# Running most of TensorE's attention units as a hardware loop, with wo read in pieces and multiplied at each layer's end

## The chip, the cores and the metric

The kernel runs on one core of one Trainium2 chip. The metric is the device time of one execution in microseconds (us). Executions of one kernel agree within about 0.15%, so a difference of some microseconds in 2600 can be read.

Names: PE is TensorE (matmul), PEld its weight load, DVE is VectorE, ACT is ScalarE, POOL is GpSimd, SP is SyncE, which issues the large loads. A "unit" is the attention of one query over one head of one batch entry: 16384 keys and values of 128 numbers, a K load and a V load of 4 MiB each. There are 64 units in each of two layers.

## The reference, cut to what matters

```python
x = A_x                                   # (2, 1, 576)
for layer in range(2):                    # written out twice in the original
    q = (layernorm(x) @ wq)               # 32 heads of 128
    p = softmax(q @ k_cache^T * Dh**-0.5) # k_cache, v_cache: (2, 32, 16384, 128) bf16
    x = x + (p @ v_cache) @ wo            # wo: (4096, 576)
    x = x + mixer_mlp(layernorm(x))       # w2 (576, 576), w3 (576, 4608), w4 (4608, 576)
# ... cut: the mixer's shifts; with one position they leave only zeros
```

Nearly all bytes are K and V: 252 loads of 4 MiB, because the last two units of layer 0 stay in SBUF and are the first two of layer 1.

## The kernel before

All loads go through a ring in SBUF of 12 slots (192 KiB a partition), in which a K or V tile takes two slots wherever they are free. The K/V tiles can thus be six deep.

```python
def pump(self):                            # Arena: issue loads while there is room
    while self.queue:
        keys, n, src, align = self.queue[0]
        best = self._place(n, align)       # the free place whose last use is oldest
        if best is None:
            return
        # ... cut: wait for the readers of what lies there, issue from SP
```

A unit's work is spread over three engines: PE transposes the first half of K (`turn`), ACT evicts it, PE multiplies it by the query (`score`); DVE takes the dot products of the other half (`dots`); then maxima, exponentials (ACT), and 128 products with V on PE (`weigh`).

```python
for i in range(U):                         # U = 64 units, all unrolled
    for c in range(NCP):                   # 8 chunks
        self.turn(l, i, c)
        # ... cut: score, unit_max and exps of unit i - 1
        if i % n == 1 and c == 6:
            self.load_wo(l, i)             # 2 heads of wo, 288 KB, from ACT's queue
        # ... cut: dots(l, i, ...) on DVE
    self.weigh(l, i - 1, 0)
    # ... cut
    self.weigh(l, i - 1, 1)
    if i % n == 0:
        self.group_out(l, i - 1)           # normalise 4 units, multiply by 2 heads of wo
    self.query_rows(l, i + 1)
    self.row_max(l, i)
```

Each engine's stream is written out in full. For PE that is 128 units of 258 matmuls, and each matmul is two instructions, a weight load and a multiply (x34571 of each in the page below).

## Time and profile before

| | before |
|---|---|
| time | 2614.34 us median of 4 (2614.12 to 2614.65) |
| bytes read | 1097.74 MB, 420 GB/s over the span |
| K/V tile after tile, usual distance of the landings | 9.71 us (4194304 bytes: 432 GB/s) |
| packets of instruction fetch, queue 8 / queue 14 | 270 of 16384 bytes / 38 of 8192 bytes |

These lines are from the page of the kernel before: busy time of the engines, the DMA engines' mean busy share and the rate in 40 slices of the span, the queues (packets, MB, share of 16 engines' span), and the chain that ended last by engine.

```profile
span 2612.6 us, 74231 instructions
PE 1560.5 (60%) x34571; PEld 1466.2 (56%) x34571; DVE 1983.0 (76%) x2751; ACT 1097.5 (42%) x1681; POOL 0.8 (0%) x10
...
DMA  9999999999999999999889999999999999999997
GB/s 409 430 428 429 428 428 428 430 427 428 428 429 427 429 428 429 429 427 430 375 366 431 427 429 427 428 428 427 432 428 427 428 429 429 428 428 429 427 428 307
...
q1 hardware_dynamic: 42600, 1088.32, 97.4%
...
q8 instruction: 270, 4.42, 0.7%
q14 instruction: 38, 0.31, 0.0%
...
DMA 67%; DVE 27%; PE 5%; issue 1%; SPq 0%; ACT 0%; DVEq 0%
```

The transfers bound it. No compute engine is over 76% busy, the DMA engines are nearly always busy, and the chain is mostly transfers. The waits of PE say the same (columns: us in total, times, longest us).

```profile
PE tps L604 <- DMA ring<-in_A_k_cache_dram: 508.7, 117, 9.9
PE ops L682 <- DMA ring<-in_A_v_cache_dram: 209.8, 115, 3.5
PE ops L682 <- issue: 47.1, 25, 3.2
```

The third line is PE waiting for nothing that the profile shows, in the middle of the products with V.

An average over 16 engines hides whether some of them are late. The trace holds 16 landing times for every K and V load, as many as the page counts DMA engines. I read each as the end of one engine's share; the records name no engine, so wherever engines are told apart below, it is read from landing times. Worked out from those records, us after the first of the 16:

```
kernel before            16 landings, us after the first
K, lands at   25.91      0 ... 0.4 (15 engines) | 1.9
V, last of layer 0,
   lands at 1299.29      0.0 0.1 0.3 0.4 0.5 1.0 | 5.4 | 10.9 | 24.8 24.8 24.9 25.0 25.0 26.4 26.9 27.0
V, last of layer 1,
   lands at 2582.13      0.0 0.3 0.3 0.3 0.4 0.8 | 5.0 | 10.1 | 23.5 23.8 24.9 25.1 25.1 25.2 25.3 25.4
```

Six engines are early, one is 5 us late, one 10 us, and eight about 25 us. The lag grows through a layer and is gone after the boundary: the last landing was 3.5 us behind the first for the load that landed at 176.8 us, 8.2 us at 367.6, 13.0 us at 637.8, 19.2 us at 918.4 and 25.8 us at 1199.6 us, and 1.6 us at 1323.5 us, after the boundary. The kernel waits for all 16 landings of a tile (its waits count in sixteens), so it runs at the pace of the eight late ones.

### The profile page before, as it was taken

The numbers are of one execution on the slowest core, as the hardware profiler recorded it, in microseconds if no ns is written. First come the engines' busy times: TensorE is split into PE (matmuls) and PEld (weight loads), VectorE is DVE, ScalarE is ACT, GpSimd is POOL, SyncE is SP. The second block draws the span as 40 slices with busy tenths as digits, with TensorE's granted clock in tenths as the row PEclk, the third lists the DMA queues.
The fourth block names the chain that finished last, engine by engine and source line by source line (L and its number), as shares of the span: only waits on it lengthen the run. The fifth ranks groups of instructions, "written<-read, shape, count | busy, mean of one in ns | idle before, by whom it ended". The sixth has DMA issues, their size and how long they took to land.

```text
span 2612.6 us, 74231 instructions
## 1 busy us (share of the span) xinstructions
PE 1560.5 (60%) x34571; PEld 1466.2 (56%) x34571; DVE 1983.0 (76%) x2751; ACT 1097.5 (42%) x1681; POOL 0.8 (0%) x10
## 2 busy tenths in 40 slices
PE   5655655656565556655567765556655655655565
PEld 4555555655555555555556755555555555555555
DVE  5777877777777777877759887777877777777775
ACT  3434443444344334434335544344434443444342
POOL 0000000000000000000000000000000000000000
PEclk8666666666666666666656666666666666666665
DMA  9999999999999999999889999999999999999997
GB/s 409 430 428 429 428 428 428 430 427 428 428 429 427 429 428 429 429 427 430 375 366 431 427 429 427 428 428 427 432 428 427 428 429 429 428 428 429 427 428 307
DMA packets 51612, 1102.50 MB, mean 422 GB/s; under 512 B 5028, under 2 KB 13288, under 8 KB 17000
## 3 DMA queue, kind: packets, MB, share of 16 engines
q1 hardware_dynamic: 42600, 1088.32, 97.4%
q10 hardware_dynamic: 8704, 9.44, 1.0%
q8 instruction: 270, 4.42, 0.7%
q14 instruction: 38, 0.31, 0.0%
HBM read 1097.74 MB, written 0.00 MB: 420 GB/s over the span
## 4 chain that ended last, share of the span: by engine, by line
DMA 67%; DVE 27%; PE 5%; issue 1%; SPq 0%; ACT 0%; DVEq 0%
DMA ring<-in_A_k_cache_dram 66%; DVE sd L637 17%; DVE prod L634 9%; PE tps L604 3%; PE misc L655 1%; DMA ring<-in_B_w_dram 1%; DMA ring<-in_A_wq_dram 1%; DVE small L657 1%; PE ops L682 0%; PE misc L515 0%; PE sps L479 0%; SPq L317 0%; PE misc L445 0%; PE misc L447 0%; DVE small L649 0%
## 5 line engine op out<-in xcount | busy, mean ns | idle before, releaser
L637 DVE TENSOR_REDUCE sd<-prod 128x8 f32<-128x1024 bf16 x1024 | 1249.4, 1220 | 35.5
L608 ACT ACTIVATE ktsb<-tps 128x1024 bf16<-128x1024 bf16 x1024 | 991.6, 1028 | 676.3 <-PE tps L604 670.8
L604 PE MATMUL tps<-ident,ring 128*128 128x128 bf16 x8192 | 829.7, 268 | 513.0 <-DMA ring<-in_A_k_cache_dram 508.7
L604 PEld LDWEIGHTS tps<-ident,ring 128*128 128x128 bf16 x8192 | 673.5, 123 | 546.5 <-DMA ring<-in_A_k_cache_dram 530.2
L634 DVE TENSOR_TENSOR prod<-ring,qb 128x1024 bf16<-128x1024 bf16 x1024 | 697.7, 681 | 11.0 <-DMA ring<-in_A_k_cache_dram 10.3
L682 PE MATMUL ops<-p,ring 128*128 128x1 bf16 x16384 | 471.6, 165 | 259.3 <-DMA ring<-in_A_v_cache_dram 209.8
L682 PEld LDWEIGHTS ops<-p,ring 128*128 128x128 bf16 x16384 | 451.5, 102 | 269.2 <-DMA ring<-in_A_v_cache_dram 219.7
L657 DVE TENSOR_REDUCE small<-misc 128x1 f32<-128x128 f32 x128 | 37.3, 292 | 489.3 <-PE misc L655 489.3
L622 PE MATMUL sps<-qt,ktsb 128*128 128x1 bf16 x8192 | 350.4, 166 | 90.8 <-ACT ktsb L608 81.5
L622 PEld LDWEIGHTS sps<-qt,ktsb 128*128 128x128 bf16 x8192 | 313.2, 102 | 131.0 <-ACT ktsb L608 129.6
L591 ACT ACTIVATE qb<-misc 128x128 bf16<-128x128 f32 x128 | 35.5, 278 | 761.7 <-PE misc L589 761.7
L655 PE MATMUL misc<-identS,small 128*128 128x128 f32 x256 | 95.5, 476 | 33.0 <-DVE small L649 33.0
L655 PEld LDWEIGHTS misc<-identS,small 128*128 128x128 f32 x256 | 69.7, 333 | 35.8 <-DVE small L649 35.8
L515 PE MATMUL misc<-otn,wobuf 128*128 128x2 bf16 x320 | 13.7, 167 | 104.2 <-DVE otn L701 104.2
L515 PEld LDWEIGHTS misc<-otn,wobuf 128*128 128x128 bf16 x320 | 11.0, 105 | 107.1 <-DVE otn L701 107.1
L668 ACT ACTIVATE p<-sps,small 128x64 bf16<-128x64 f32 x128 | 40.6, 317 | 19.2 <-DVE small L657 19.2
L589 PE MATMUL misc<-ident,qt 128*128 128x128 bf16 x128 | 34.8, 272 | 18.0 <-DVE xa L711 7.8
L668 ACT ACTIVATE p<-sd,small 128x64 bf16<-128x64 f32 x128 | 45.4, 355 | 0.0
L645 DVE TENSOR_REDUCE small<-sps 128x1 f32<-128x64 f32 x128 | 27.6, 215 | 0.0
L668 ACT ACTIVATION_READ_ACCUMULATOR p<-sps,small 128x1 f32 x128 | 27.1, 212 | 0.0
L647 DVE TENSOR_REDUCE small<-sd 128x1 f32<-128x64 f32 x128 | 26.7, 208 | 0.0
L668 ACT ACTIVATION_READ_ACCUMULATOR p<-sd,small 128x1 f32 x128 | 26.5, 207 | 0.0
(70 smaller groups left out, 183.9 us busy)
## 6 DMA issues: line engine op xcount, KB each, us to landing
ring<-in_A_k_cache_dram SPq DMA_DIRECT2D x126, 4096.0 KB, 43.8
ring<-in_A_v_cache_dram SPq DMA_DIRECT2D x126, 4096.0 KB, 53.5
wobuf<-in_A_wo_dram ACTq DMA_DIRECT2D x32, 288.0 KB, 24.7
ring<-in_B_w_dram SPq DMA_DIRECT2D x8, 1152.0 KB, 47.9
ring<-in_A_wq_dram SPq DMA_DIRECT2D x8, 1024.0 KB, 11.2
ring<-in_B_w_dram SPq DMA_DIRECT2D x2, 2160.0 KB, 42.3
ring<-in_B_w_dram SPq DMA_DIRECT2D x2, 1728.0 KB, 26.9
ring<-in_B_w_dram SPq DMA_DIRECT2D x3, 576.0 KB, 40.6
```

What stands on the lines that cost most here:

```text
L589: self.pe(lambda pe: pe.matmul(self.misc[:, 0:128], lhsT=bcast(self.qt[:, u:u + 1], 128), rhs=self.ident[:, :], start=True, stop=True), r= ...
L591: self.act(lambda a: a.activation(out=self.qb[q][:, :], in_=self.misc[:, 0:128], func=ACT.Copy), r=["P:misc"], w=[f"qb{q}"])
L604: ins = pe.transpose(self.tps[b][:, j * 128:(j + 1) * 128], kt[:, (j0 + j) * 128:(j0 + j + 1) * 128], self.ident[:, :])
L608: self.act(lambda a: a.activation(out=self.ktsb[k][:, :, :].rearrange("p a b -> p (a b)"), in_=self.tps[b][:, :], func=ACT.Copy), r=[f"P:t ...
L622: ins = pe.matmul(self.sps[sp][:, col:col + 1], lhsT=self.ktsb[k][:, j, :], rhs=self.qt[:, u:u + 1], start=True, stop=True)
L634: self.dve(lambda v: v.tensor_tensor(out=self.prod[d][:, :, :], in0=k3, in1=bcast_mid(self.qb[q][:, :], self.CH), op=ALU.mult), r=[*res, f ...
L637: self.dve(lambda v: v.tensor_reduce(out=self.sd[q][:, o:o + self.CH], in_=self.prod[d][:, :, :], axis=AX.X, op=ALU.add), r=[f"prod{d}"], ...
L645: self.dve(lambda v: v.tensor_reduce(out=self.m1[:, q:q + 1], in_=self.sps[q][:, 0:n], axis=AX.X, op=ALU.max), r=[f"P:sps{q}"], w=[f"m1{q}"])
L655: self.pe(lambda pe: pe.matmul(self.misc[:, 128:256], lhsT=bcast(self.m[:, q:q + 1], 128), rhs=self.identS[:, :], start=True, stop=True), ...
L657: self.dve(lambda v: v.tensor_reduce(out=self.bias[:, q:q + 1], in_=self.misc[:, 128:256], axis=AX.X, op=ALU.max, negate=True), r=["P:misc ...
L668: self.act(lambda a, c0=c0, c1=c1, src=src, part=part: a.activation(out=self.p[q][:, c0:c1], in_=src, func=ACT.Exp, bias=self.bias[:, q:q ...
L682: ins = pe.matmul(self.ops[g][:, col:col + 1], lhsT=vt[:, j * 128:(j + 1) * 128], rhs=self.p[q][:, h * self.TB + j:h * self.TB + j + 1], s ...
```

## The change

Its intent is to take PE's instruction stream out of the memory traffic: most units are run by PE as a hardware loop whose body is two units. The body is written once, with fixed addresses, which is why the layout changes too. SBUF's ring becomes three fixed thirds, each holding one unit (K and V), and units alternate between two of them; the other third holds wo, which is now read in pieces during a layer, from SP's queue instead of ACT's, and multiplied at the layer's end. The query column and the output column, whose address would change with the unit, go through small fixed buffers. A wait whose value grows with the turn is computed in a register.

```diff
+    with eng.Fori(0, n) as turn:                      # PE only
+        for o, waits in self._fold(turns):
+            self._run(eng, o, [(s, v + turn * d if d else v) for s, v, d in waits])
 ...
+    def place(self, l, i):                            # which third unit i lives in
+        if l == 0:
+            return 2 if i == self.U - 1 else i % 2
+        return (2, 0, 1, 2, 0)[i] if i < 5 else (2, 1)[i % 2]
 ...
+    def query(self, l, i):                            # ACT copies the unit's query column
+        self.act(... out=self.qcur[:, q:q + 1], in_=self.qt[:, u:u + 1] ...)
 ...
     def weigh(self, l, i, h):
-        ins = pe.matmul(self.ops[g][:, col:col + 1], ...)
+        ins = pe.matmul(self.ops[q][:, 0:1], ...)
+        if h == 1:
+            self.dve(... tensor_copy(out=self.o[:, u:u + 1], in_=self.ops[q][:, 0:1]) ...)
 ...
     def attention(self, l):
+        first, last = 2 + 4 * l, U - 6
+        self.s.loops.append((l * U + first, (last - first) // 2, 2))
         for i in range(U):
-            if i % n == 1 and c == 6:
-                self.load_wo(l, i)
+            if i == last + 1:
+                self.project_pieces(l, range(self.n_wo - 1))   # 7 pieces, 28 heads
 ...
-                if i % n == 0:
-                    self.group_out(l, i - 1)
+            if i == U - 2:
+                self.project_pieces(l, [self.n_wo - 1])        # 1 piece, 3 heads
 ...
-        self.group_out(l, U - 1)
+        self.project_last(l)                                   # the last head
# cut: the loads' fixed places, wo's cuts, a place of the mixer's shift term, and the small buffers
```

Layer 0 loops over 28 pairs of units and layer 1 over 26, so 20 of the 128 units stay unrolled.

## The prediction

2614 less about 31 us (26.9 - 10.9 and 25.4 - 10.1, from the landings) is 2583 us. That the body stays resident, meaning here that its turns fetch nothing, and the 72% for it were the author's estimate; the cost of the other case, which the upper end of the range (2630 us) was to cover, was not shown. A "block" is a packet of 16384 bytes: in the page before, 34571 multiplies and 34571 weight loads came with 270 packets, 256 instructions a packet, and the "4.2 blocks" of the loop body and the 62 fetches that remain are estimates from that. The expectations of e5 to e8 count 128 instructions for 8192 bytes, an estimate by the same ratio.

> **What bounds the kernel now.** Data transfer. The page gives the hardware queue 97.4% of the 16 DMA engines' span, and the chain of waits is 67% transfers, nearly all K loads; a busy stretch moves 428 to 430 GB/s. DVE (76%) and PE (60%) wait for K each unit.
>
> The slowest DMA engine sets the pace[...].[...] The K load that landed at 25.9 us has its 16 landings within 1.9 us; the last V of layer 0 (1299.3 us) has six early ones within 1.1 us, one 5.4 us behind, one 10.9 us behind, and eight 24.8 to 27.0 us behind. Layer 1 repeats it (25.4 us at 2582.1). So eight engines carry extra work and everything waits for them. The extra is instruction fetch: queue 8 moves 270 packets of 16384 bytes (4.42 MB), and PE's 69,300 records are 271 blocks of 256. About 131 fetches per layer over eight engines are 16.4 each; 24 us of lag over that is about 1.46 us a fetch, the size of the step seen about every 80 us, when the gap between tile landings goes from 9.71 to about 11.2 us. The two middle engines fit the 38 packets of 8192 bytes on queue 14, for the other engines.
>
> **What the change does.** PE loops over 28 pairs of units in layer 0 and 26 in layer 1; 20 of 128 units stay unrolled. A unit is 258 matmuls, 516 instructions; the loop body is about 1,070, or 4.2 blocks.[...]
>
> If resident, about 62 fetches remain (3 per engine and layer, about 4.4 us). Then the slowest engine is the one with other engines' fetches, 10.9 us behind, which the change leaves. The gain is therefore not all 26 us per layer but 26.9-10.9 and 25.4-10.1, about 31 us in all.
>
> **Costs, mostly hidden.** Look-ahead falls from six K/V tiles to four while the third part holds wo. In the timeline K's place frees 16.4 us after it lands, and its successor must start by 29 us: about 12.7 us in hand. PE gets about 25 register operations per pair and a branch; it ends a unit's work about 15.3 us into a 19.4 us period without fetch stalls (its 47 us of "issue" waits before the V products should shrink). DVE adds a copy (about 0.2 us) and does row maxima later; it ends near 18.4 of 19.4 us. wo has the same bytes and 1152-byte runs: 0.83 us per 288 KB, unchanged. Boundary dependences (w4 after w3, wq after w4, K after wq) are as before.
>
> **Prediction.** 2614-31 = 2583 us, range 2572 to 2630: 72% resident, 28% that the body is fetched again each turn[...]. Faster by over 2%: 0.04; within 2%: 0.92; slower: 0.04.
>
> **What would show it.** Right: queue 8 near 60 packets, under 1.1 MB; the eight engines' lag at layer end under 5 us; last landing about 11 us behind the first; tile gaps 9.71 us without the 11.2 us steps; K waits of PE as long as now. Wrong: 270 or more packets; PE stalls of 3 to 4 us each pair; or DVE/PE, not K, ending the waits because four tiles are too few (GB/s below 425 in loop slices), or queue 14's fetches spreading differently.

## The result

The changed kernel takes 2590.86 us (median of 4, 2590.72 to 2591.52) against 2614.34 us. Ratios here are the mean time of one kernel's fast runs over the mean of the other's fast runs of the same rounds, so not quite the ratio of the medians quoted. This one is 0.9911 (95% interval 0.9893 to 0.9928), so it is within 2% but 0.9% faster. The prediction, 2583 us with a range of 2572 to 2630 us, held; it was 8 us too low.

The same lines of the page after:

```profile
span 2588.8 us, 75423 instructions
PE 1539.4 (59%) x34519; PEld 1451.9 (56%) x34519; DVE 1977.0 (76%) x2775; ACT 1111.4 (43%) x1809; POOL 0.8 (0%) x10
...
DMA  9999999999999999999998999999999999999998
GB/s 415 429 427 432 431 431 430 429 434 431 431 430 431 430 431 432 430 432 401 423 395 359 433 432 430 431 430 431 433 430 432 430 432 430 430 433 432 429 424 343
...
q1 hardware_dynamic: 51224, 1097.76, 99.1%
q8 instruction: 59, 0.97, 0.1%
q14 instruction: 39, 0.32, 0.0%
...
DMA 54%; DVE 37%; PE 8%; issue 1%; ACT 0%; SPq 0%; DVEq 0%
```

PE executes about as many matmuls as before (x34519), yet queue 8 moved 59 packets instead of 270. Between 89.5 and 1170.9 us, while layer 0 loops, it moved none: the turns ran without fetching their body again. The rate in looped slices went from about 428 to 431 GB/s. The page's share of 0.7% for queue 8 would never have suggested it, but by the landings those 0.7% lay on eight of the 16 engines.

PE's waits after:

```profile
PE tps L665 <- DMA buf<-in_A_k_cache_dram: 665.8, 115, 9.2
PE ops L738 <- DMA buf<-in_A_v_cache_dram: 180.4, 115, 2.7
PE ops L738 <- issue: 13.2, 9, 3.1
```

The waits on "issue" fell with the fetches. PE waits longer for K than before (508.7 to 665.8 us). That is not the loop's doing: the same layout without the loop (e1 below) shows 662.3 us. Most of what went is the wait for DVE before each small product with wo, 104.2 us in 32 waits before and 13.1 us in 5 after; K sets the pace, so the time freed turns up as waiting for K.

```
kernel after             16 landings, us after the first
V, lands at 1115.46      0.0 0.1 0.2 0.5 0.7 0.9 1.8 1.9 2.0 2.0 2.0 2.1 2.1 2.2 4.3 9.1
V, last of layer 0,
   lands at 1282.52      0.0 0.1 0.2 0.2 0.3 0.3 0.4 0.9 1.5 1.7 1.7 1.7 1.7 1.8 2.0 4.7
V, last of layer 1,
   lands at 2558.47      0.0 0.2 0.4 0.5 0.6 0.6 1.8 1.8 1.8 1.9 1.9 1.9 2.1 2.6 2.7 8.4
```

The group of eight is gone. One engine is still late and now sets the pace. In the loops, the distances of about 11.2 us that remain each follow the landing of a piece of wo (the one that landed at 760.2 us, for example, before the distance of 11.20 us at 769.9 us), so they are not instruction fetch.

What was given back is at the start of layer 1. There the trace has one distance of 20.7 us between two landings (1410.29 and 1431.01 us). SP's issues around it, in order of time (start us, us, what):

```profile
1384.72 0.43 SPq L356 DMA_DIRECT2D buf<-in_A_v_cache_dram  x1
1417.37 0.33 SPq L356 DMA_DIRECT2D buf<-in_A_k_cache_dram  x1
1417.74 0.43 SPq L356 DMA_DIRECT2D buf<-in_A_v_cache_dram  x1
```

The K load of unit 7 goes where K of unit 5 lies. That K landed at 1390.90 us, but DVE read its last chunk only at 1416.66 us, as DVE's timeline shows:

```profile
1416.66 0.68 DVE L694 TENSOR_TENSOR prod<-buf,qb 128x1024 bf16<-128x1024 bf16 x1
1417.38 1.22 DVE L697 TENSOR_REDUCE sd<-prod 128x8 f32<-128x1024 bf16 x1
```

DVE is behind here because layer 1 starts with two units that need no load and with a bubble while wq arrives: its first products of the layer start at 1321.18 us, and from there it works almost without a pause, a unit every 16.5 us. That is read from the timeline. Before, six tiles of room absorbed that: the same stretch has no such gap.

### The profile page after: what moved, and what is told of

Read it like the earlier page. It is cut to its first block, busy times and chain, and to the rows that moved or that the text cites. A ratio compares the mean times of both kernels' runs of the same rounds, so it can differ in the third digit from the quotient of the medians.

```text
span 2588.8 us, 75423 instructions
## 1 busy us (share of the span) xinstructions
PE 1539.4 (59%) x34519; PEld 1451.9 (56%) x34519; DVE 1977.0 (76%) x2775; ACT 1111.4 (43%) x1809; POOL 0.8 (0%) x10
## 4 chain that ended last, share of the span: by engine, by line
DMA 54%; DVE 37%; PE 8%; issue 1%; ACT 0%; SPq 0%; DVEq 0%
DMA buf<-in_A_k_cache_dram 50%; DVE sd L697 23%; DVE prod L694 13%; PE tps L665 4%; DMA buf<-in_A_v_cache_dram 2%; PE misc L715 2%; DVE small L717 1%; DMA buf<-in_A_wq_dram 1%; PE ops L738 1%; PE misc L575 0%; DMA buf<-in_B_w_dram 0%; PE sps L539 0%; SPq L370 0%; PE misc L505 0%; DVE small L709 0%
## 5 line engine op out<-in xcount | busy, mean ns | idle before, releaser
L665 PE MATMUL tps<-ident,buf 128*128 128x128 bf16 x8192 | 833.2, 269 | 668.5 <-DMA buf<-in_A_k_cache_dram 665.8
L665 PEld LDWEIGHTS tps<-ident,buf 128*128 128x128 bf16 x8192 | 676.3, 123 | 698.2 <-DMA buf<-in_A_k_cache_dram 687.3
L694 DVE TENSOR_TENSOR prod<-buf,qb 128x1024 bf16<-128x1024 bf16 x1024 | 697.5, 681 | 10.8 <-DMA buf<-in_A_k_cache_dram 9.9
L738 PE MATMUL ops<-p,buf 128*128 128x1 bf16 x16384 | 467.5, 165 | 194.7 <-DMA buf<-in_A_v_cache_dram 180.4
L738 PEld LDWEIGHTS ops<-p,buf 128*128 128x128 bf16 x16384 | 448.7, 102 | 205.8 <-DMA buf<-in_A_v_cache_dram 188.7
L682 PE MATMUL sps<-qcur,ktsb 128*128 128x1 bf16 x8192 | 350.5, 166 | 91.3 <-ACT ktsb L669 83.1
L682 PEld LDWEIGHTS sps<-qcur,ktsb 128*128 128x128 bf16 x8192 | 314.6, 102 | 130.2 <-ACT ktsb L669 128.3
L645 ACT ACTIVATE qcur<-qt 128x1 bf16<-128x1 bf16 x128 | 29.1, 227 | 19.3 <-DVE qt L582 19.3
L650 PE MATMUL misc<-ident,qcur 128*128 128x128 bf16 x128 | 34.2, 267 | 1.6 <-ACT qcur L645 1.1
L745 DVE COPY o<-ops 128x1 f32<-128x1 f32 x128 | 18.9, 148 | 9.3 <-PE ops L738 9.3
```

The lines of the kernel that those rows point to most:

```text
L645: self.act(lambda a: a.activation(out=self.qcur[:, q:q + 1], in_=self.qt[:, u:u + 1], func=ACT.Copy), r=["qt"], w=[f"qcur{q}"])
L650: self.pe(lambda pe: pe.matmul(self.misc[:, 0:128], lhsT=bcast(self.qcur[:, q:q + 1], 128), rhs=self.ident[:, :], start=True, stop=True), ...
L665: ins = pe.transpose(self.tps[b][:, j * 128:(j + 1) * 128], kt[:, (j0 + j) * 128:(j0 + j + 1) * 128], self.ident[:, :])
L682: ins = pe.matmul(self.sps[sp][:, col:col + 1], lhsT=self.ktsb[k][:, j, :], rhs=self.qcur[:, sp:sp + 1], start=True, stop=True)
L694: self.dve(lambda v: v.tensor_tensor(out=self.prod[d][:, :, :], in0=k3, in1=bcast_mid(self.qb[q][:, :], self.CH), op=ALU.mult), r=[*res, f ...
L738: ins = pe.matmul(self.ops[q][:, 0:1], lhsT=vt[:, j * 128:(j + 1) * 128], rhs=self.p[q][:, h * self.TB + j:h * self.TB + j + 1], start=(h ...
```

## The experiments

The theory (A): the gain is PE's instruction fetch taken off eight DMA engines, and the slowest DMA engine sets the pace. Rivals: the gain comes from the layout and wo (B); a fetch costs time only because the engine that fetches waits for its instructions (I). The theory about the shortfall (C): two rotating thirds are too few at the start of layer 1; its rival (D): the loop itself costs time on PE or DVE. A table of all runs:

| run | queue 8 / 14 packets | median us | ratio to before |
|---|---|---|---|
| before | 270 / 38 | 2614.34 | 1 |
| changed kernel | 59 / 39 | 2590.86 | 0.9911 |
| e1_unrolled | 270 / 39 | 2620.83 | 1.0022 |
| e2_loop_layer0 | 161 / 39 | 2604.97 | 0.9962 |
| e3_body_of_four | 317 / 39 | 2631.90 | 1.0066 |
| e4_three_places | 67 / 39 | 2582.33 | 0.9875 |
| e5_copy_on_act | 67 / 39 | 2581.47 | 0.9872 |
| e6_dve_loop | 67 / 24 | 2574.49 | 0.9846 |
| e7_pool_30 | 67 / 72 | 2582.92 | 0.9879 |
| e8_pool_60 | 67 / 101 | 2603.28 | 0.9955 |

All gave the correct result, and each was timed in three rounds beside the kernel before, which took 2614.44 to 2614.68 us in these rounds, so that runs of different rounds can be compared.

### e1_unrolled: the changed kernel without its loop

```diff
-        self.s.loops.append((l * U + first, (last - first) // 2, 2))
+        pass
```

> The changed kernel with the hardware loop taken out again: same fixed thirds, same wo pieces, PE fully unrolled. Theory A (the gain is PE's instruction fetch taken off eight DMA engines): queue 8 is back at about 270 packets, eight landings of the last V load of each layer are 15 to 25 us behind the first, and the time is back at or above the kernel before, about 2618 us (2614 plus about 11 us for the stall at the start of layer 1, less some us for cheaper wo loads), range 2608 to 2626. Rival B (the gain comes from the new layout and the wo pieces): at most 2600 us.

Measured: 2620.83 us, queue 8 back at 270 packets.

```profile
q8 instruction: 270, 4.42, 0.7%
...
PE ops L738 <- issue: 35.2, 24, 3.2
```

Theory A holds and B falls. With layout and wo held the same, the loop is worth 2620.83 - 2590.86 = 30.0 us. The layout with its wo pieces costs 2620.83 - 2614.60 = 6.2 us (2614.60 is the kernel before in these rounds). One part of the expectation was wrong: the eight late landings at the layers' ends were 6 to 8.4 us behind, not 15 to 25. The lag grew to 11.2 us by 527 us and then stayed near 10 to 12.5. Four tiles of room seem to allow no more: the early engines run out of issued loads and wait, which costs the late ones nothing (read from the landings, not tested). So with short look-ahead this spread no longer measures how much extra work the late engines carry.

### e2_loop_layer0: half the dose

```diff
-        self.s.loops.append((l * U + first, (last - first) // 2, 2))
+        if l == 0:
+            self.s.loops.append((l * U + first, (last - first) // 2, 2))
```

> The hardware loop in layer 0 only, layer 1 unrolled: half the dose. Theory A: queue 8 at about 160 packets, the last V of layer 0 with a spread near 5 to 10 us, that of layer 1 near 25 us or as far as four tiles allow, time about 2606 us (2591 plus about 15), range 2600 to 2611. Rival B: 2591 us.

Measured: 2604.97 us with 161 packets. The last V of layer 0 lands at 1282.71 us (1282.52 in the changed kernel), that of layer 1 at 2572.56 us (2558.47): the 14 us are lost in the layer that is unrolled. The time follows the dose: 15.9 us and 109 packets less than e1, where the changed kernel has 30.0 us and 211 packets less.

### e3_body_of_four: a body that is fetched at every turn

```diff
-        self.s.loops.append((l * U + first, (last - first) // 2, 2))
+        self.s.loops.append((l * U + first, (last - first) // 4, 4))
```

> The loop body holds four units instead of two: about 2140 instructions, 8.4 blocks of 16 KiB. Theory A1[...]: each turn fetches its body again, queue 8 is at 260 packets or more, PE shows waits on issue of some us at each turn's start, the lag of eight engines returns, time 2612 to 2630 us. Rival A2 (what is kept is larger, or what counts is only that it is a loop): queue 8 at about 75 packets and 2591 to 2594 us.

Measured: 2631.90 us, 1.9 us above the expected range, and 317 packets.

```profile
q8 instruction: 317, 5.19, 0.8%
...
PE sps L682 <- issue: 32.8, 30, 2.2
PE tps L665 <- issue: 15.7, 9, 7.0
```

It is a loop all the same, and it is slower than the kernel before, and 11.1 us slower than the same layout unrolled (e1). Each turn of four units fetches about 10 packets, where the kernel before fetches about 8 in the same time (the 27 turns make 47 packets more than e1). From e1 to the changed kernel a packet was worth 0.14 us (30.0 us over 211), so the 47 packets more than e1's make about 7 us, an estimate; the remaining 4 us may be PE's own stalls, which this run does not separate. So it is not looping that pays but a body that is not fetched again: the one of 4.2 blocks fetched nothing for 1081 us (the changed kernel), the one of 8.4 blocks about 10 packets a turn. No body between those sizes was run, so where the change comes, and why, was not shown.

### e4_three_places: longer look-ahead at the start of layer 1

```diff
-        return (2, 0, 1, 2, 0)[i] if i < 5 else (2, 1)[i % 2]
+        return (2, 0, 1)[i % 3] if i < 9 else (1, 2)[i % 2]
...
-                j, r = divmod(i - 7, gap)
+                j, r = divmod(i - 7 - 4 * l, gap)
...
-        first, last = 2 + 4 * l, U - 6
+        first, last = 2 + 8 * l, U - 6
```

> Layer 1 uses all three buffer thirds for its first nine units (wo pieces four units later, the loop starts at unit 10). Theory C (the 7.5 us by which the change fell short of the forecast are a stall of 11 us at the start of layer 1, where the K load of unit 7 waits for the K of unit 5 because only two thirds rotate and DVE is behind): no gap of over 12 us between K/V landings after the fifth unit of layer 1, time about 2580 us, range 2577 to 2584. Rival D (the shortfall is the loop's own cost, register operations and branches on PE, or the slower end of a unit on DVE): 2591 us within 2 us.

Measured: 2582.33 us, 8.5 us under the changed kernel; the 20.7 us gap is gone. Busy time by stretch, for the 40 us around it, first in the changed kernel, then in this run (the last two columns are the DMA engines' share and GB/s):

```profile
1400.00:1440.00 40.00, 27.57 (x572) 26.32 (x573) 36.43 (x54) 20.34 (x32) 0.00 (x0) 0.63 0.76 316
```

```profile
1400.00:1440.00 40.00, 27.56 (x570) 26.36 (x571) 36.58 (x54) 20.38 (x32) 0.00 (x0) 0.63 1.00 429
```

DVE is equally busy in both; only the transfers idle in the first. Theory C holds. For D nothing is left that these runs can resolve: this kernel still has the loop's register operations and DVE's later row maxima. Of the gap's 11.0 us, 8.5 came back; the loop of layer 1 is two pairs shorter here (67 packets for 59), which may have taken part of the rest (not tested).

### e5_copy_on_act and e6_dve_loop: the engine that is late now

In the changed kernel the last late engine falls back by about 1 us each 120 us. DVE's fetches fit that: packets of queue 14 start at 291.6, 411.9, 532.2, 657.3 and 778.0 us. To test it, DVE is looped as well. Its one address that changes with the unit, in the copy of the output column, is moved to ACT; e5 is that move alone, on top of e4.

```diff
-            self.dve(lambda v: v.tensor_copy(out=self.o[:, u:u + 1], in_=self.ops[q][:, 0:1]),
+            self.act(lambda a: a.activation(out=self.o[:, u:u + 1], in_=self.ops[q][:, 0:1], func=ACT.Copy),
# e6 only:
-                def run(eng, items=plan[e], loops=self.loops if e == "tensor" else ()):
+                def run(eng, items=plan[e], loops=self.loops if e in ("tensor", "vector") else ()):
```

> Control for the next run: the three-thirds kernel (2582.3 us) with the small copy of each unit's output moved from DVE to ScalarE, nothing else. Both theories: 2582 us within 2 us, queue 14 near 39 packets; DVE's fetches fall by about one block, ScalarE's rise by one.

> As the control, and DVE runs the same pairs of units as a hardware loop too: 2788 instructions become 720, so about 16 fewer packets of 8192 bytes on queue 14. Theory F (with PE looped, the slowest DMA engine is the one that serves DVE's instruction fetches, about 1 us for each, some 9 a layer): queue 14 near 23 packets, no landing alone 6 to 9 us behind the others before the end of layer 0, time about 2572 us, range 2568 to 2578. Rival G (the remaining lag has another source, or it is hidden): 2582 us. Rival H (waits through registers make DVE, which has about 1 us a unit in hand, the limit): slower than 2582 us, and DVE busy share up or its idle time no longer ended by K.

Measured: 2581.47 us for the control and 2574.49 us with DVE looped, 7.0 us less. The queue's line in the control, then in the loop:

```profile
q14 instruction: 39, 0.32, 0.0%
```

```profile
q14 instruction: 24, 0.20, 0.0%
```

15 packets of 8 KB, 0.12 MB of 1099, were worth 7.0 us. Near 1100 us the last landing of a tile was 9.2 us behind the first in the control and 4.8 us here, and the last V of layer 0 lands at 1277.37 instead of 1281.98 us. Theory F holds. Rival H falls: in the timeline DVE's pairs of operations still follow each other every 1.85 us. DVE's waits on "issue" were 0.2 us in all in the kernel before, too little to explain a gain, so this is also a first sign against rival I. The kernel of e6 beats both the kernel before and the changed one (ratio to before 0.9846).

### e7_pool_30 and e8_pool_60: fetch alone

POOL has almost no work in this kernel (0.8 us). Giving it idle memsets adds fetch traffic. It is not quite free of waits: because the memsets read `m`, DVE gets 126 wait instructions for POOL. But no DVE time during the attention is put down to POOL, and DVE is busy for 1977.2 us in e7 and e8 against 1976.7 in e4. On top of e4:

```diff
+        def f(g):
+            for j in range(30):                      # e8: 60
+                ins = g.memset(self.pad[:, j:j + 1], 0.0)
+            return ins
+        self.last_pad = self.s.op("gpsimd", f, [f"m{q}"], ["pad"], self.last_pad and [self.last_pad] or [])
```

> The three-thirds kernel (2582.3 us) with 30 idle memsets of one element a unit on GpSimd, which otherwise has no work: 3840 instructions, about 30 more packets of 8192 bytes on queue 14, and no wait added for PE, DVE or ScalarE. Theory A/F (a fetch costs time on the DMA engine that serves it, about 1 us for 8 KB, and the slowest engine sets the pace): about 15 us of lag a layer if GpSimd has an engine of its own, beside 9 for DVE's, so about 12 us more in all, 2594 us, range 2586 to 2606 (the top if it shares an engine with DVE's fetches). Rival I (fetch costs time only where the engine that fetches has to wait for its instructions): 2582 us within 2 us.

> The same with 60 memsets a unit, 7680 instructions, about 60 more packets of 8192 bytes. Theory A/F: about 30 us of lag a layer on one engine, 2624 us, range 2606 to 2640, and about twice the rise of the run before over its own threshold; last landings of the K/V loads by one engine alone. Rival I: 2582 us within 2 us.

Measured: 2582.92 us with 30 memsets (2586 to 2606 expected, so a miss) and 2603.28 us with 60 (2606 to 2640 expected, so a miss too). From the page of e8:

```profile
PE 1540.4 (59%) x34519; PEld 1452.7 (56%) x34519; DVE 1977.2 (76%) x2775; ACT 1110.3 (43%) x1809; POOL 260.9 (10%) x7690
...
q14 instruction: 101, 0.83, 0.1%
```

The landings say why the first dose did nothing:

```
                         16 landings, us after the first
e7, lands at 1086.43     0.0 ... 2.0 (13 engines) | 4.5 | 8.9 | 9.0
e8, lands at 1086.81     0.0 ... 0.8 (14 engines) | 3.6 | 12.1
```

In e7 two engines were equally late, where e5 had one, 9.2 us behind at 1086.77 us. In e8 one engine alone sets the pace. By the landings POOL's fetches load an engine of their own, at about 0.7 us each (8.9 us over the 12.7 blocks it had run through, an estimate), not the 1 us that I had taken from DVE's. The first dose only drew level with the engine that was already the slowest. The second passed it. With 0.7 us, 30 fetches a layer make about 21 us against DVE's 9, so 12 us more in each of two layers: about 2606 us, an estimate made after the runs, against 2603.28 measured. Rival I, whose number e7 taken alone would have confirmed, falls with e8: no other engine spends time waiting for POOL, and yet 21 us were lost.

## Why the prediction was right, and what was off

- That the body stays resident (72% in the prediction): right. 59 packets against about 62 forecast, and none while layer 0 loops. (The prediction's "3 per engine and layer" is a slip: 62 over eight engines and two layers is 3.9. Its number does not rest on it.)
- That the gain is limited by the next slowest engine, "about 31 us in all": right. e1 measures the loop alone at 30.0 us, and e6 shows that the engine left over is the one with DVE's fetches.
- "Costs, mostly hidden": this is the term that was mis-sized. I put the cost of the shorter look-ahead at zero from a steady unit ("about 12.7 us in hand") and called the boundary the same as before. The copy that DVE adds took 0.148 us (x128), against "about 0.2 us". The layout costs 6.2 us (e1), and its largest part is the stall of 11 us at the start of layer 1 (8.5 us come back in e4). The margin vanishes where DVE is behind the loads, which the trace of before did not show because six tiles hid it.
- "wo ... unchanged": slightly off. A piece of 576 KB lengthens the distance of two tiles by 1.49 us, where two of the old 288 KB loads took 1.66 us. Over both layers that is about 3 us in the change's favour, an estimate from these distances.
- "last landing about 11 us behind the first" at layer end: it was 9.1 us at 1115 us and 10.0 us at 1184 us, but 4.7 and 8.4 us at the ends. The early engines had run out of loads, as in e1; that part is argued from the landings, not tested.
- "the eight engines' lag at layer end under 5 us" was right (about 2 us), and so was the disappearance of the fetch's 11.2 us steps, one about every 80 us; steps of 10.7 us, which fit DVE's fetches, remained, and the pieces of wo made steps of about 11.2 us of their own, 14 in all, which the prediction did not have.
- "K waits of PE as long as now" was wrong (508.7 to 665.8 us), without consequence for the time: the layout took PE's waits for DVE away (662.3 us of K waits without the loop, in e1), and K still set the pace.

## What to carry to other kernels

When transfers bound a kernel, look at the slowest DMA engine and not at the mean: compare the first and the last landing of a load, and watch that difference grow. Here instruction fetch took time on the DMA engines like the loads' own transfers: 0.7% of 16 engines' span for 270 packets, about 1.1 us each. PE's long stream as a loop whose body was not fetched again was worth 30.0 us of 2620.83, or 1.1% (e1 against the changed kernel), for 3.45 of 1102.50 MB, or 0.3% of the bytes; a loop whose body was fetched at every turn was 11.1 us worse than unrolling (e3 against e1). Removing the slowest engine's load only paid down to the next slowest (DVE's fetches, another 7.0 us in e6), and buffers given up for it must be checked where compute is behind the loads, not only in the steady state.
